# A chain's lower part on GpSimd instead of VectorE, and a smaller booked cost of a new chain, in a two-layer attention and MLP kernel

## The chip, the cores and the metric

The kernel runs on one core of a Trainium2 chip. The metric is the device time of one execution in microseconds. The profile is of one execution, taken by the hardware profiler; times in it are counted from the start of its span. Engines are called PE (TensorE), PEld (its weight loads), DVE (VectorE), ACT (ScalarE), POOL (GpSimd) and SP (SyncE).

## The reference

Two rounds of an attention block and an MLP, each with a layer norm ahead of it and a residual sum behind it, on 2048 rows of 512 in bf16; 32 heads of 16, a hidden width of 1792, the same weights in both rounds:

```python
def _A_ref(x, wqkv, wo):          # x: 1 x 2048 x 512, H = 32, Dh = 16
    qkv = (x @ wqkv) ...          # split into q, k, v per head
    scores = jnp.einsum("bhqd,bhkd->bhqk", q, k) * (Dh ** -0.5)
    p = _softmax(scores, axis=-1)
    o = jnp.einsum("bhqk,bhkd->bhqd", p, v)
    return o ... @ wo

def _B_ref(x, w1, w2):            # w1: 512 x 1792
    return maximum(x @ w1, 0) @ w2

x = x + _A_ref(_layernorm(x), A_wqkv, A_wo)
x = x + _B_ref(_layernorm(x), B_w1, B_w2)
x = x + _A_ref(_layernorm(x), A_wqkv, A_wo)
x = x + _B_ref(_layernorm(x), B_w1, B_w2)
```

## The kernel before

The exponential of the scores is the bulk of the work: 2 x 32 heads x 2048 x 2048 values. They are computed with the keys on the partitions, in blocks of 128 keys by 512 queries (narrower chunks of queries near the end of the second round are packed to 512 columns). A **slot** is three such blocks in three banks of PSUM, of which there are two sets (`ps_s`, slots alternate). In every slot TensorE makes the scores (line 1694), ScalarE takes the exponential of two or three of the blocks into `e` (line 1707), and TensorE multiplies the result by the values into `ps_o` (line 1163, the function `pv`; the values carry a column of ones, which gives the softmax's sum). The scores of slot n+2 go into the banks of slot n, so they wait until its readers are done.

In many slots VectorE takes the third block in ScalarE's place. It uses an approximation that reads a linear function of the score as the bits of a bf16 number. For each block, `lin` = max(score + bias, 0) as int16 (line 1283, PSUM to SBUF, 512 columns). Three blocks make a **chain** (`GROUP` = 3), whose 1536 columns are then shifted up and down: `up` = max(lin + 41, 0) and `down` = max(lin - 41, 0) (both in line 1335, the local function `shifted`). TensorE adds up all three for each block: `lin` and `up` against the values (`vaug`), and `down` against values scaled by 1.55 (`vscaled`). Where no scaled values are there for all blocks of the chain (`p["scaled"]` false), VectorE scales `down` itself (line 1340, `weigh`), and TensorE uses `vaug`. So a block done in this way needs three matmuls against the values instead of one. There are four buffers of `lin` (`NP`) and two each of `up` and `down` (`NC`).

The order of all engines' work is written out when the program is built, by a planner with its own clocks: `now_pe`, `now_dve`, the ends of the exponentials, the time at which SP's queue and GpSimd come free (`sp_free`, `pool_free`), and a table `made` that holds for each result the engine and the planned time. For every slot it puts the matmuls that fit before the scores are needed; `run_dve` then fills VectorE up to the planned end of the exponential before: first the steps that must be done (`musts`: `lin`, and the copies out of `ps_o`), then results of other matmuls, then tasks of `dve_q` whose dependences are planned as met. A task of a chain has the lowest rank unless its head is nearly over. Nothing of this order changes at run time; engines wait for one another by semaphores.

A chain is begun in a slot only if `lin`'s buffer is free, TensorE's other work isn't behind (`pace`, `press`), and

```python
queued = sum(t["cost"] for t in dve_q if "chain" in t)
ends = max(now_dve[0] + others, now_pe[0] + FILL) + SPREAD * (queued + CHAIN)
if asked or now_dve[0] + waiting < now_pe[0] + BACKLOG:
    ... ends < now_pe[0] + till * QS * 0.84 - 1300.0
```

where `till` counts the blocks of the head that are still to come, `SPREAD` is 1.3 and `CHAIN` is the booked cost of a chain in ns. A `down` task has to wait for `("free", "down", n - NC)`: the last matmul on the buffer's content of two chains before.

GpSimd has little to do: the small steps between a norm's statistics and its reciprocal root (lines 587 to 595, nine steps of 128x4 values, 17 times), some copies and fills at the start (lines 207, 236, 243), and the DMAs that spread the reciprocals of the softmax sums (line 1117). `recip` and `rstd` book these on `pool_free`.

Of the kernel before, what the change touches and what calls it, by code (L numbers as in the profile page):

```python
# [17 lines left out]
ALU = mybir.AluOpType  # L18
# [7 lines left out]
def kernel(  # L26
# [10 lines left out]
    nc = tc.nc  # L37
# [28 lines left out]
    THIRD, WEIGHT, SUM = 41.0, 1.55, 3.63198  # L66
# [1 line left out]
    UNIT = 128.0  # L68
    EXP_BIAS = (127.0 - math.log2(SUM)) * UNIT
    GROUP = 3  # L70
    CHAIN = 1500.0
    FILL = 4000.0
    SOON = 1500.0
    NP = 4
    NC = 2
# [4 lines left out]
    PE_TO_DVE, DVE_TO_PE, ACT_TO_PE, PE_TO_ACT = 220.0, 180.0, 160.0, 222.0  # L80
# [6 lines left out]
    BOTH = 4  # L87
    WHOLE = 4
    STARTS, MORE, ORDER = {}, {}, {}
    X_AT = (8.3, 8.5, 9.5, 10.6, 11.0, 11.4, 11.8, 12.1, 12.5, 12.8, 13.3, 14.0)  # L90
    WQ_AT, WV_AT = {0: 0.0, 1: 10600.0, 2: 16000.0, 3: 17400.0}, 10200.0
    FIRST_TRANSPOSE = 1600.0
# [24 lines left out]
    def sb(shape, dt, name):  # L117
        return persist.tile(shape, dt, name=name)
# [40 lines left out]
    up = [sb([P, GROUP * QS], I16, f"up{n}") for n in range(NC)]  # L159
    down = [sb([P, GROUP * QS], I16, f"down{n}") for n in range(NC)]  # L160
# [125 lines left out]
    now_dve = [0.0]  # L286
# [5 lines left out]
    made = {}  # L292

    def mark(key, engine="dve", lag=0.0):
        made[key] = (engine, (now_pe if engine == "pe" else now_dve)[0] + lag)
# [3 lines left out]
    pool_free = [0.0]  # L299
# [27 lines left out]
    def pe_start(kind, ready=0.0):  # L327
        return max(now_pe[0] + (SWITCH if MODE[mode[0]] != MODE[kind] else 0.0), ready)
# [19 lines left out]
    dve_q = []  # L348
    maker = {}
# [3 lines left out]
    def task(cost, fn, makes=(), deps=(), place=None):  # L353
        t = {"cost": cost, "fn": fn, "makes": makes, "deps": deps}
        dve_q.insert(len(dve_q) if place is None else place, t)
        maker.update({k: t for k in makes})
# [921 lines left out]
    def dve_block(half, taken, src, ex, recent):  # L1278
# [3 lines left out]
        def first_step():  # L1282
            first = nc.vector.tensor_scalar(  # L1283
                out=lin[which][:, half * QS : (half + 1) * QS], in0=src, scalar1=EXP_BIAS,
                scalar2=0.0, op0=ALU.add, op1=ALU.max,
            )
            tc.declare_no_dep(
                first.ins, ex.ins, reason="both only read the scores, and in different banks"
            )
            for earlier in recent:  # L1290
                tc.declare_no_dep(
                    first.ins, earlier,
                    reason="the scores read here were written after it, and are waited for",
                )
            step1_end[slot[0]] = now_dve[0]
            readers[slot_no % 2].append((first.ins, (W - 1,)))
            mark(line_key)
            if half == GROUP - 1:
                chain(pairs[-1])
# [26 lines left out]
    def chain(p):  # L1326
        key, n = p["key"], p["n"]
        line = lin[n % NP][:]
        p["scaled"] = all(
            ("third", sg["l"], kb) in made for us in p["blocks"] for sg, kb, g in us  # L1330
        )
        quick = 67 + 0.2591 * GROUP * QS

        def shifted(out, by):
            nc.vector.tensor_scalar(  # L1335
                out=out, in0=line, scalar1=by, scalar2=0.0, op0=ALU.add, op1=ALU.max
            )

        def weigh(x):
            nc.vector.tensor_scalar(out=x, in0=x, scalar1=WEIGHT, scalar2=None, op0=ALU.mult)  # L1340

        above, below = up[n % NC][:], down[n % NC][:]
        first = ("lower",) if not p["scaled"] else ("down",)
        steps = [
            (("up",), lambda: shifted(above, THIRD), [("free", "up", n - NC)]),
            (first, lambda: shifted(below, -THIRD), [("free", "down", n - NC)]),
        ]
        if not p["scaled"]:
            steps.append((("down",), lambda: weigh(below.bitcast(BF16)), [key + first]))
        for of, fn, deps in steps:  # L1350
            task(quick, fn, [key + of], [d for d in deps if d[0] != "free" or d[2] > 0])
            maker[key + of]["chain"] = p
# [12 lines left out]
    for e in range(2):  # L1365
        nc.vector.tensor_reduce(
            out=mask[e],
# [4 lines left out]
            out=qmask[:, e : e + 1],  # L1372
# [4 lines left out]
            out=qmask[:, e : e + 1], in0=qmask[:, e : e + 1], scalar1=SCALE * LOG2E * UNIT, scalar2=None,  # L1377
            op0=ALU.mult,
# [3 lines left out]
    for n in range(2):  # L1382
# [3 lines left out]
        for i in rows:  # L1386
            nc.vector.bn_aggr(out=mv[0][:, i, :], in_=stats[0][:, i, :])
        nc.vector.tensor_scalar(
            out=half_va[n][:], in0=mv[0][:, rows.start : rows.stop, 1], scalar1=EPS, scalar2=None,
            op0=ALU.add,  # L1390
        )
        nc.gpsimd.tensor_tensor(
            out=half_ya[n][:], in0=half_va[n][:], in1=masks[:, 4:5].to_broadcast((P, HALF)),
# [6 lines left out]
    def head_bank(n, w):  # L1400
        return ps_s[n][:, w, :] if n < 2 else ps_f[:]
# [53 lines left out]
    for e in range(2):  # L1455
        uses(
            nc.vector.tensor_scalar(
                out=qbuf[0][:, e, :], in0=head_bank(0, 0), scalar1=qmask[:, e : e + 1],
                scalar2=None, op0=ALU.mult,
# [8 lines left out]
    made["wv",] = "dve", WV_AT  # L1468
    for n, when in enumerate(X_AT):
        made["x", TPC + n] = "dve", 1000.0 * when  # L1470
# [71 lines left out]
    while units:  # L1542
# [5 lines left out]
        for (sg, kb, g), *_ in banked:  # L1548
            if sg["n"] not in seen:
                seen.add(sg["n"])  # L1550
                n = sg["n"] + 1
# [14 lines left out]
        if len(banked) == W and (  # L1566
# [5 lines left out]
            elif asked != 0 and lin_free(pair_no[0] + 1 - NP) and (  # L1572
# [12 lines left out]
                )  # L1585
                ends = max(now_dve[0] + others, now_pe[0] + FILL) + SPREAD * (queued + CHAIN)
                if asked or now_dve[0] + waiting < now_pe[0] + BACKLOG:
# [93 lines left out]
        start = pe_start("s", s_ready)  # L1681
# [7 lines left out]
        for _ in range(times):  # L1689
            pe_run("s", 1, s_ready)  # L1690
            for a, (sg, kb, g) in sorted(zip(place, now), key=in_turn):
# [6 lines left out]
                    start=True, stop=True, tile_position=(32 * g, 0),  # L1698
# [6 lines left out]
        while len(pend) == NE:  # L1705
            force_v()
        ex = nc.scalar.activation(  # L1707
            out=eb[:, 0 : place[m]], in_=b[:, 0 : place[m]], func=ACTF.Exp,
# [33 lines left out]
        if to_load and no >= FIRST_LOAD and sp_free[0] < now_pe[0]:  # L1742
            out, in_ = to_load.popleft()
# [28 lines left out]
    def at_bank(b):  # L1772
        n, w = b
        return ps_s[n][:, w, :] if n < 2 else (ps_f, ps_o)[n - 2][:]
# [68 lines left out]
    for i in rows:  # L1843
        nc.vector.bn_aggr(out=mv[n_last][:, i, :], in_=stats[n_last][:, i, :])
    nc.vector.tensor_scalar(
        out=va_[n_last][:, 0:n_rows], in0=mv[n_last][:, 0:n_rows, 1], scalar1=EPS, scalar2=None,
        op0=ALU.add,
    )
    nc.gpsimd.tensor_tensor(
        out=ya_[n_last][:, 0:n_rows], in0=va_[n_last][:, 0:n_rows],  # L1850
# [29 lines left out]
    for ft in range(NF + LOOK):  # L1880
# [4 lines left out]
        if ft < NF:  # L1885
# [6 lines left out]
            if ft % 2:  # L1892
                out = nc.scalar.activation(out=ht[ft][:, at_column : at_column + width], in_=at_bank(b)[:, 0:width], func=ACTF.Relu)
            else:
                out = nc.vector.tensor_scalar(
                    out=ht[ft][:, at_column : at_column + width], in0=at_bank(b)[:, 0:width],
                    scalar1=0.0, scalar2=None, op0=ALU.max,
                )
# [42 lines left out]
```

## Time and profile before

| | us |
|---|---|
| median of 3 runs (1455.55 to 1455.71) | 1455.7 |
| the profiled execution | 1454.99 |
| its span | 1453.1 |
| ACT busy | 1426.5 |
| PE busy | 1368.8 |
| DVE busy | 1307.2 |
| POOL busy | 96.7 |

The span runs from the first to the last instruction; the profiled execution's own time lies 1.9 us above it. Busy time is summed over the whole span, with stages that have different limits. The granted TensorE clock is 1.00 throughout. The page's line of a group gives its source line, engine, operation, what is written and read with shapes, the count, busy us in all, the mean in ns, and the idle time of the engine ahead of it with what ended it. One line of the source can stand for several tiles: 1335 for `up` and `down`, 1163 for all products with the values.

### The profile page before, as it was taken

What the parts mean: (1) busy time and instruction counts of PE and PEld (TensorE: products, weight loads), DVE (VectorE), ACT (ScalarE), POOL (GpSimd) and SP (SyncE); (2) the same over time, 40 slices, a digit from 0 to 9 for tenths busy, and PEclk for the clock granted to TensorE, in tenths of its full rate; (3) what the DMA queues carried; (4) which work ended last, traced back from release to release, by engine and by line L of the source; (5) the groups of instructions that cost most, each with busy time, mean ns of one, the idle gap of its engine ahead of it and who ended that gap; (6) DMA issues with size and microseconds to landing.
All of it is one profiled execution on the core that took longest, in us unless ns stands there. A gap on an engine that the chain in (4) does not pass through costs nothing.

```text
span 1453.1 us, 47371 instructions
## 1 busy us (share of the span) xinstructions
PE 1368.8 (94%) x20884; PEld 511.7 (35%) x20885; DVE 1307.2 (90%) x2414; ACT 1426.5 (98%) x1386; POOL 96.7 (7%) x249
## 2 busy tenths in 40 slices
PE   8999899999999999999999999889999999999898
PEld 3222222222232223222222223223234444545665
DVE  7969999999999999999599987899989799998864
ACT  7999999999999999999999999999999999999996
POOL 5000001001010011000000000001001010010000
PEclk9999999999999999999999999999999999999999
DMA  5201101101012100210101100000110211223030
GB/s 146 82 5 24 25 10 31 42 14 31 10 24 50 27 17 10 46 39 17 24 5 26 35 5 5 10 15 18 45 39 20 54 29 39 51 45 69 11 70 18
DMA packets 135502, 46.59 MB, mean 32 GB/s; under 512 B 119904, under 2 KB 132512, under 8 KB 135296
## 3 DMA queue, kind: packets, MB, share of 16 engines
q1 hardware_dynamic: 128240, 37.44, 10.8%
q0 software_dynamic: 5568, 5.15, 1.9%
q8 instruction: 163, 2.67, 0.8%
q10 hardware_dynamic: 1488, 0.98, 0.2%
q14 instruction: 43, 0.35, 0.1%
HBM read 24.38 MB, written 2.10 MB: 18 GB/s over the span
## 4 chain that ended last, share of the span: by engine, by line
ACT 76%; PE 17%; DVE 5%; issue 1%; DMA 0%; DVEq 0%; ACTq 0%
ACT e L1707 76%; PE ps_s L1694 5%; PE ps_f L542 5%; PE ps_o L1163 5%; DVE lin L1283 2%; PE ps_s L1778 1%; DVE down L1335 1%; DVE up L1335 1%; DVE vaug L776 0%; DVE x L909 0%; DVE ht L869 0%; DVE stats L578 0%; DMA x<-in_A_x_dram 0%; DVE u L1055 0%; PE ps_o L542 0%
## 5 line engine op out<-in xcount | busy, mean ns | idle before, releaser
L1707 ACT ACTIVATE e<-ps_s 128x1024 bf16<-128x1024 f32 (+1 forms) x1366 | 1418.0, 1207 | 7.9 <-PE ps_s L1694 5.4
L1283 DVE TENSOR_SCALAR lin<-ps_s 128x512 int16<-128x512 f32 x993 | 663.7, 683 | 34.8 <-PE ps_s L1694 29.0
L1694 PE MATMUL ps_s<-q,ktp 32*128 32x512 bf16 (+2 forms) x6346 | 578.6, 321 | 52.9 <-ACT e L1707 47.3
L1163 PE MATMUL ps_o<-e,vaug 128*32 128x512 bf16 (+2 forms) x4318 | 389.4, 326 | 8.1 <-DVE r L1055 3.5
L1694 PEld LDWEIGHTS <-ktp 32*128 32x128 bf16 x6346 | 183.5, 91 | 523.4 <-issue 507.0
L1163 PEld LDWEIGHTS <-vaug 128*32 128x32 bf16 x7153 | 177.4, 95 | 225.2 <-issue 194.6
L1335 DVE TENSOR_SCALAR up<-lin 128x1536 int16<-128x1536 int16 x331 | 182.0, 550 | 14.9 <-PE ps_o L1163 13.6
L1335 DVE TENSOR_SCALAR down<-lin 128x1536 int16<-128x1536 int16 x331 | 181.6, 549 | 0.5 <-PE ps_o L1163 0.5
L1163 PE MATMUL ps_o<-up,vaug 128*32 128x512 bf16 (+2 forms) x1314 | 168.7, 328 | 0.9 <-issue 0.9
L1163 PE MATMUL ps_o<-lin,vaug 128*32 128x512 bf16 (+2 forms) x1314 | 158.5, 328 | 2.4 <-DVE u L1055 0.7
L1163 PE MATMUL ps_o<-down,vscaled 128*32 128x512 bf16 (+2 forms) x1107 | 152.3, 335 | 0.0
L542 PE MATMUL ps_f<-w,ht 128*32 128x512 bf16 x1680 | 135.0, 382 | 0.9 <-DVE x L909 0.7
L542 PE MATMUL ps_f<-xnT,w 128*32 128x512 bf16 (+1 forms) x1792 | 124.3, 355 | 1.2 <-DVE ht L869 0.5
L542 PE MATMUL ps_f<-xnT,wkq 128*32 128x512 bf16 (+2 forms) x1376 | 101.6, 353 | 7.7 <-DVE vaug L776 2.2
L869 DVE TENSOR_SCALAR ht<-ps_f 128x512 bf16<-128x512 f32 (+1 forms) x111 | 74.1, 667 | 19.6 <-PE ps_f L542 12.6
L1163 PEld LDWEIGHTS <-vscaled 128*32 128x32 bf16 x1107 | 50.2, 96 | 18.0 <-issue 10.7
L542 PEld LDWEIGHTS <-w 128*32 128x32 bf16 x1792 | 41.3, 95 | 39.6 <-issue 28.6
L542 PEld LDWEIGHTS <-ht 128*32 128x32 bf16 x1680 | 37.2, 95 | 39.8 <-issue 27.1
L542 PEld LDWEIGHTS <-wkq 128*32 128x32 bf16 x1376 | 33.3, 95 | 42.4 <-issue 33.2
L587 POOL TENSOR_TENSOR ta<-stats 128x4 f32<-128x4 f32 (+2 forms) x17 | 4.8, 281 | 604.0 <-DVE stats L578 604.0
L578 DVE BATCH_NORM_STATS2 stats<-x 128x6 f32<-128x512 bf16 x63 | 42.3, 682 | 1.4 <-DMA x<-in_A_x_dram 1.1
L542 PE MATMUL ps_f<-wv,xnT 128*32 128x512 bf16 x480 | 38.6, 383 | 3.1 <-DVE vaug L776 1.7
(140 smaller groups left out, 583.5 us busy)
## 6 DMA issues: line engine op xcount, KB each, us to landing
w<-in_B_w_dram SPq DMA_DIRECT2D x144, 128.0 KB
q<-xn SPq DMA_DIRECT2D x48, 64.0 KB
out_dram<-x SPq DMA_DIRECT2D x15, 128.0 KB
x<-in_A_x_dram SPq DMA_DIRECT2D x14, 128.0 KB
u<-r POOLq DMA_DIRECT2D x12, 128.0 KB, 4.6
ktp<-in_B_w_dram SPq DMA_DIRECT2D x10, 128.0 KB
u<-ht POOLq DMA_DIRECT2D x6, 128.0 KB, 4.7
r<-r SPq DMA_DIRECT2D x6, 128.0 KB
```

The costliest lines, as they stand in the source:

```text
L542: nc.tensor.matmul(out[cols], lhsT[:, cols], rhs, start=i % k == 0, stop=i % k == k - 1, tile_position=(0, 32 * g), skip_group_check=True,)
L578: nc.vector.bn_stats(out=stats[ln_n(tag)][:, i, :], in_=x_t[tt][:])
L587: pool.tensor_tensor(out=t1, in0=st[:, :, 1], in1=st[:, :, 4], op=ALU.subtract)
L869: nc.vector.tensor_scalar(out=out, in0=sums, scalar1=0.0, scalar2=None, op0=ALU.max)
L1163: nc.tensor.matmul(ps_o[32 * g : 32 * g + 32, 0 : sg["w"]], values[:, 4 * sg["T"] + g, 2 * e : 2 * e + 32], rhs, start=g not in sg["begun" ...
L1283: first = nc.vector.tensor_scalar(out=lin[which][:, half * QS : (half + 1) * QS], in0=src, scalar1=EXP_BIAS, scalar2=0.0, op0=ALU.add, op1 ...
L1335: nc.vector.tensor_scalar(out=out, in0=line, scalar1=by, scalar2=0.0, op0=ALU.add, op1=ALU.max)
L1694: score = nc.tensor.matmul(b[:, a : a + sg["w"]], kt[32 * g : 32 * g + 32, kc : kc + P], qbuf[sg["n"] % 2][32 * g : 32 * g + 32, sg["e"], ...
L1707: ex = nc.scalar.activation(out=eb[:, 0 : place[m]], in_=b[:, 0 : place[m]], func=ACTF.Exp, scale=1.0 / (LOG2E * UNIT),)
L1778: uses(nc.tensor.matmul(out, lhsT, rhs, start=first, stop=last), b, needs=needs)
```

## The change

When an `up` has been put on VectorE, the new function `up_step` looks whether GpSimd can make `down` out of it: max(up - 82, 0), which is the same number as max(lin - 41, 0). It does so where the chain's blocks all have scaled values, the buffer of `down` is planned to be free, and GpSimd could start within 600 ns (`POOL_WAIT`) of VectorE's planned time. Then the `down` task is taken out of VectorE's queue, GpSimd is booked for 2300 ns (`POOL_DOWN`) from a start 150 ns (`POOL_LAT`) behind `up` or later, and `down` is marked as made at the end of that. Else VectorE makes it as before. `CHAIN` goes from 1500 to 1100. `POOL_SPACE` is not used.

```diff
-    CHAIN = 1500.0
+    CHAIN = 1100.0
...
+    POOL_DOWN, POOL_LAT, POOL_WAIT, POOL_SPACE = 2300.0, 150.0, 600.0, 0.0
...
+        def up_step():
+            shifted(above, THIRD)
+            free = ("free", "down", n - NC)
+            if not p["scaled"] or n > NC and free not in made:
+                return
+            start = max(now_dve[0] + POOL_LAT, pool_free[0], made.get(free, (0, 0.0))[1] + DVE_TO_PE)
+            if start > now_dve[0] + POOL_WAIT:
+                return
+            nc.gpsimd.tensor_scalar(
+                out=below, in0=above, scalar1=-2.0 * THIRD, scalar2=0.0, op0=ALU.add, op1=ALU.max
+            )
+            pool_free[0] = start + POOL_DOWN
+            dve_q.remove(maker[key + ("down",)])
+            mark(key + ("down",), lag=pool_free[0] - now_dve[0])
...
         steps = [
-            (("up",), lambda: shifted(above, THIRD), [("free", "up", n - NC)]),
+            (("up",), up_step, [("free", "up", n - NC)]),
             (first, lambda: shifted(below, -THIRD), [("free", "down", n - NC)]),
```

## The prediction

> **What bounds the kernel now.** I read the page's busy line first, then the groups by form, the chain that ended last, and the table by stretches of 50 us.
>
> ```profile
> PE 1368.8 (94%) x20884; PEld 511.7 (35%) x20885; DVE 1307.2 (90%) x2414; ACT 1426.5 (98%) x1386; POOL 96.7 (7%) x249
> ...
> ACT 76%; PE 17%; DVE 5%; issue 1%; DMA 0%; DVEq 0%; ACTq 0%
> ```
>
> ScalarE is busy for 98% of the span and is 76% of the chain that ended last: the exponentials set the time. The groups by form (count, busy us, mean ns, idle before) say how VectorE shortens them:
>
> ```profile
> L1707 ACT ACTIVATE e<-ps_s 128x1024 bf16<-128x1024 f32 x993 | 937.6, 1094 | 4.3 <-PE ps_s L1694 3.5
> L1283 DVE TENSOR_SCALAR lin<-ps_s 128x512 int16<-128x512 f32 x993 | 663.7, 683 | 34.8 <-PE ps_s L1694 29.0 <-ACT e L1707 0.4
> L1707 ACT ACTIVATE e<-ps_s 128x1536 bf16<-128x1536 f32 x372 | 525.7, 1509 | 3.6 <-PE ps_s L1694 1.8 <-PE ps_o L1163 0.8
> L1335 DVE TENSOR_SCALAR up<-lin 128x1536 int16<-128x1536 int16 x331 | 182.0, 550 | 14.9 <-PE ps_o L1163 13.6
> L1335 DVE TENSOR_SCALAR down<-lin 128x1536 int16<-128x1536 int16 x331 | 181.6, 549 | 0.5 <-PE ps_o L1163 0.5
> ```
>
> There are 1366 slots: 993 in which VectorE takes one block of 512 (three make a chain, so 331 chains), 372 in which ScalarE does all 1536 (and one narrow). Start to start in the timeline an exponential takes 904 ns at 1024 and 1331 ns at 1536 (medians), so one block moved is worth 0.427 us and one chain 1.28 us of ScalarE. Is VectorE what limits the number of chains? Not everywhere (columns: stretch, length, then PE, PEld, DVE, ACT, POOL busy):
>
> ```profile
> 250.00:300.00 50.00, 48.83 (x619) 14.06 (x612) 49.80 (x90) 50.00 (x53) 2.53 (x4) 1.00 0.21 47
> 450.00:500.00 50.00, 49.43 (x625) 14.74 (x626) 49.74 (x90) 50.00 (x52) 1.21 (x2) 1.00 0.17 39
> 850.00:900.00 50.00, 47.41 (x600) 15.16 (x597) 36.72 (x65) 48.24 (x44) 2.60 (x9) 1.00 0.02 7
> ```
>
> In some 19 of 29 such stretches (950 us, VectorE 48.3 of 50 on average) VectorE is full; in the others (850:900) the planner's other conditions hold chains back, and a freer VectorE brings nothing. In the full stretches TensorE has only 0.5 to 4 us left too.
>
> **How much goes to GpSimd.** Of 331 chains 40 have the weighing step (line 1340) and stay. For the other 291 I laid the diff's conditions on the starts in the trace: the last read of the `down` buffer two chains before lies behind, and GpSimd, 2.3 us per piece, comes free within 0.6 us. 239 pass. A `down` starts 0.46 us before what follows it (550 ns long, its end overlaps), so 239 x 0.46 = 110 us leave VectorE.
>
> **What the planner does with it.** `CHAIN` 1100 for 1500 lowers the expected end of a new chain by 1.3 x 400 = 520 ns, and the removed tasks lower its VectorE clock; so it begins k more chains. Each costs VectorE three `lin` at a pitch of 0.60, an `up` of 0.46 and a quarter of a `down`: 2.4 us. If the planner keeps VectorE at its present 96.6% in the full stretches (77% of the chains, so 85 us leave there): 918 - 85 + 2.4k = 0.966 x (950 - 1.28k), k = 23. ScalarE: -29 us; VectorE: +55 us. TensorE: six more matmuls of four abreast per chain, 1.5 x 0.216 = 0.32 us, 7 us in all, which its gaps hold except in stretches such as 450:500; there the new chain makes TensorE late, at most those 7 us.
>
> **The price of one piece on GpSimd.** No row shows a 128x1536 arithmetic step there. Nearest from below is the fill (0.83 ns per element beyond 0.1 us: 1.4 us for 1536); nearest in kind is the copy, which also reads and writes:
>
> ```profile
> L207 POOL COPY wkq<-w 128x512 bf16<-128x512 bf16 x6 | 4.4, 764 | 4.8 <-DMA w<-in_A_wqkv_dram 4.8
> L236 POOL MEMSET q<- 128x1024 bf16 x1 | 1.0, 951 | 0.0
> ```
>
> The copy's slope is (764 - 190)/512 = 1.12 ns (190 is what the smallest GpSimd steps take), 1.9 us for 1536; back to back copies start 0.68 us apart, which gives 2.0. I take 2.0, with 1.4 and 2.3 (the diff's `POOL_DOWN`) as ends.
>
> **What it does to VectorE meanwhile.** This decides the case. Where one of VectorE's int16 steps runs, GpSimd's small steps get longer (start, length):
>
> ```profile
> 223.00 0.54 DVE L1335 TENSOR_SCALAR up<-lin 128x1536 int16<-128x1536 int16 x1
> 223.17 0.43 POOL L587 TENSOR_TENSOR ta<-stats 128x4 f32<-128x4 f32 x1 [46.35 <-DVE stats L578]
> 223.46 0.56 DVE L1335 TENSOR_SCALAR down<-lin 128x1536 int16<-128x1536 int16 x1
> 223.69 0.39 POOL L588 TENSOR_TENSOR ta<-ta 128x4 f32<-128x4 f32 x1
> ...
> 1195.38 1.33 POOL L1117 DMA_DIRECT2D u<-r  x2 [3.14 <-DVE down L1335]
> 1195.77 0.69 DVE L1340 TENSOR_SCALAR down<-down 128x1536 bf16<-128x1536 bf16 x1
> ```
>
> Alone they take 0.20 us. Here each ends 0.05 to 0.06 us after the VectorE step: the second comer waits for the first. The other way, GpSimd first, shows in small: an `up` that began 16 ns behind a GpSimd step took 595 ns instead of 550, and the weighing at 1195.77 took 687. Against it: an `up` at 226.16 inside a 1.04 us power step of four elements per row took 548; but that step hardly moves data. A piece of 1536 elements moves data from end to end, so I take it that a VectorE int16 or bf16 step from SBUF to SBUF (`up`, `down`, `xn`, lines 629 and 1137) that starts within it waits for its end. `lin` reads PSUM, and I charge it nothing.
>
> The Trainium skill, "SBUF — State Buffer", section "Who interferes with whom", says just this: VectorE and GpSimd share one pair of ports as an exclusive lock, and against a VectorE instruction in a two-port mode whoever is first has it for the whole instruction. The rows above agree for GpSimd as second comer; for a long GpSimd step no run here shows it. By that rule the blocking below is in full; by the 45 ns of the small steps alone it would be nearly nothing.
>
> I took the VectorE starts of the trace, removed the 239 `down`s, moved up what stood right behind each, and let every such step wait for a GpSimd piece that had begun. At 2.0 us per piece 130 steps wait, 117 us together; at 1.4 us 84 steps, 51 us; at 2.3 us 180 steps, 172 us. The waits are spread evenly, about 9 us per 100. So of the 110 us freed, VectorE gets nothing at 2.0.
>
> Who is behind the waiting `up`? The next `lin`, and behind it TensorE's scores two slots on: from the end of a `lin` to those scores is 0.55 us in the median, and the scores end 0.30 us before ScalarE needs them. A wait of up to 0.85 us is covered; the 130 waits exceed that by 32 us in sum (5 at 1.4, 60 at 2.3). That is the lower bound. Upper bound: VectorE is already full, catches up nothing, and the 950 us last as long as it needs: 918 - 85 + 55 + 0.77 x 117 = 978, at 98.5% busy 993, so +43.
>
> **Sum**, on the profiled execution (1454.99 us; its span is 1453.1, and 1.9 lies around it; the median of the runs is 1455.7): between 32 - 29 = +3 and +43. I take the middle, +23: 1478. With the ends of the price: 1.4 us gives 5 - 29 = -24, 2.3 us gives (918 - 85 + 55 + 132)/0.985 - 950 = +86.
>
> What is moved past other queues: 46 DMA issues and 17 groups of nine small steps stand in GpSimd's queue and can now stand 2 us behind a piece. The planner books both (`pool_free`), and the ones for `r` are planned 10 us ahead; I cost that at nothing; without that cover a row's normalisation starts 2 us late, 17 times, of which TensorE sees little. SP's queue is not touched.
>
> **Rivals.**
> - Faster: the piece is near the fill's 1.4 us, or does not hold VectorE. Then the 23 chains pay: -24 to -29, 1429. For it: the 548 ns `up` within the power step, and 9 `up`s in 250:290 that mostly lie 3 to 5 us apart. Against: the waits of GpSimd above.
> - Slower by another way: the piece takes over 2.6 us or waits itself, so that it ends later than the planner booked. TensorE's order is fixed, and it reads a `down` 1.9 us after its start in the median (a quarter under 1.2); with a piece 0.5 us over its booking about half of 239 readers wait 0.5 us, 60 us, beside 60 or more of VectorE's: about 1540. It decides from 2.5 us on. GpSimd had to wait behind a VectorE step in only 29 of the 239 cases, 0.4 us each, which speaks against it.
> - Hardly anything happens: conditions fail far more often than in my count, or chains don't increase and waits fall under the cover: 1455.
>
> **Chances.** Forecast 0.55, faster 0.30, late pieces 0.10, nothing 0.05. A measurement of this kernel tells 0.2%, 2.9 us, from no change; the lower bound of the forecast (+3) puts 0.03 of it there. So faster 0.30, same 0.08, slower 0.62. The forecast's own range is 1457 to 1515 (+60, some way from +43 towards the +86 of the longest piece). For 8 in 10 the low end goes down into the faster case, to 1430, which leaves about a third of it (0.10) below; the late pieces (0.10) are left out above.
>
> **What would show it.** In the changed kernel: some 240 `down` rows on POOL of about 2.0 us; `lin` rows some 70 above 993; the shorter exponentials as many more; `up` rows on DVE with a maximum of 2 us or more instead of 595 ns, and a mean above 0.8; new idle time of ScalarE before line 1707, released by TensorE, and of TensorE's scores waiting for `lin`. Wrong: if `up` stays at 550 ns beside running GpSimd pieces, the lock is not there and the time falls. If `up` is long and the time still falls, the cover of 0.85 us was larger than I say. If `down` on POOL lasts over 2.5 us, the second rival is at work.

## The result and the profile after

The changed kernel takes 2062.95 us (median of 4 runs, 2062.38 to 2064.91) against 1455.7: the ratio is 1.4172, 95% interval 1.4151 to 1.4193. The forecast was slower by 23 us; it is slower by 607. The page of the changed kernel, its busy line and the two lines of the groups by form for ScalarE:

```profile
PE 1630.7 (79%) x20735; PEld 533.3 (26%) x20735; DVE 1726.2 (84%) x2299; ACT 1466.3 (71%) x1388; POOL 915.5 (44%) x401
```

```profile
L1723 ACT ACTIVATE e<-ps_s 128x1024 bf16<-128x1024 f32 x1014 | 985.4, 1043 | 472.2 <-PE ps_s L1710 454.2 <-PE ps_o L1164 9.2 <-issue 3.5
L1723 ACT ACTIVATE e<-ps_s 128x1536 bf16<-128x1536 f32 x351 | 495.2, 1476 | 105.6 <-PE ps_s L1710 93.0 <-PE ps_o L1164 5.5 <-issue 5.3
```

The work moved off ScalarE is there: 21 more short exponentials (1014 for 993). But ScalarE, which never waited before (8 us in the same two lines), now stands idle for 578 us, and 547 of them end with the scores from TensorE. VectorE is busy 419 us longer although it does 115 instructions fewer. The groups by form say where:

```profile
L1348 POOL TENSOR_SCALAR down<-up 128x1536 int16<-128x1536 int16 x152 | 823.0, 5414 | 930.9 <-DVE up L1336 734.3 <-PE ps_o L1164 74.7 <-PE ps_s L1710 51.7
L1284 DVE TENSOR_SCALAR lin<-ps_s 128x512 int16<-128x512 f32 x1014 | 678.5, 684 | 153.8 <-PE ps_s L1710 149.0 <-ACT e L1723 0.5
L1336 DVE TENSOR_SCALAR up<-lin 128x1536 int16<-128x1536 int16 x338 | 473.8, 1408 | 38.5 <-PE ps_o L1164 22.2 <-issue 9.0 <-POOL down L1348 4.2
L1336 DVE TENSOR_SCALAR down<-lin 128x1536 int16<-128x1536 int16 x186 | 222.5, 1196 | 8.2 <-PE ps_o L1164 8.1
```

GpSimd made 152 of 338 `down`s and took 5.41 us for each, not 2.0. `up` went from a mean of 550 ns to 1408, the `down`s left on VectorE from 549 to 1196, and `lin`, which reads PSUM, stayed at 684 (683 before). At 550 ns the 338 `up`s would take 186 us and the 186 `down`s 102: 408 us of VectorE's time are waiting that the profile counts as busy. One place in the timeline (start, length):

```profile
381.85 5.37 POOL L1348 TENSOR_SCALAR down<-up 128x1536 int16<-128x1536 int16 x1 [5.39 <-DVE up L1336]
382.49 0.69 DVE L1284 TENSOR_SCALAR lin<-ps_s 128x512 int16<-128x512 f32 x1 [0.80 <-PE ps_s L1710]
383.60 0.69 DVE L1284 TENSOR_SCALAR lin<-ps_s 128x512 int16<-128x512 f32 x1 [0.42 <-PE ps_s L1710]
384.21 3.42 DVE L1336 TENSOR_SCALAR up<-lin 128x1536 int16<-128x1536 int16 x1
387.55 0.67 DVE L1284 TENSOR_SCALAR lin<-ps_s 128x512 int16<-128x512 f32 x1
```

Two `lin` pass beside the piece unhindered; the `up` of the next chain starts 2.36 us into it and ends 0.41 us after it (387.63 against 387.22). The `lin` behind the `up` is 3 us late, and the scores that go into its bank with it. The list of waits (us, times, longest) has ScalarE's waits for scores and, since TensorE's order is fixed, a second, smaller wait that wasn't there before:

```profile
ACT e L1723 <- PE ps_s L1710: 547.2, 368, 5.8
PE ps_o L1164 <- POOL down L1348: 109.2, 57, 3.4
```

The granted TensorE clock, 1.00 before, averages 0.85, and TensorE is busy for 262 us more with about as many products.

### The profile page after: what moved, and what is told of

Same layout as the page of the kernel before. It is cut to its first block, busy times and chain, and to the rows that moved or that the text cites. A ratio compares the mean times of both kernels' runs of the same rounds, so it can differ in the third digit from the quotient of the medians.

```text
span 2063.1 us, 47311 instructions
## 1 busy us (share of the span) xinstructions
PE 1630.7 (79%) x20735; PEld 533.3 (26%) x20735; DVE 1726.2 (84%) x2299; ACT 1466.3 (71%) x1388; POOL 915.5 (44%) x401
## 5 line engine op out<-in xcount | busy, mean ns | idle before, releaser
L1723 ACT ACTIVATE e<-ps_s 128x1024 bf16<-128x1024 f32 (+1 forms) x1366 | 1457.1, 1154 | 577.9 <-PE ps_s L1710 547.2
L1348 POOL TENSOR_SCALAR down<-up 128x1536 int16<-128x1536 int16 x152 | 823.0, 5414 | 930.9 <-DVE up L1336 734.3
L1710 PE MATMUL ps_s<-q,ktp 32*128 32x512 bf16 (+2 forms) x6130 | 666.1, 363 | 107.1 <-DVE lin L1284 77.6
L1336 DVE TENSOR_SCALAR up<-lin 128x1536 int16<-128x1536 int16 x338 | 473.8, 1408 | 38.5 <-PE ps_o L1164 22.2
L1164 PE MATMUL ps_o<-e,vaug 128*32 128x512 bf16 (+2 forms) x4285 | 440.8, 362 | 11.8 <-DVE r L1056 3.4
L1164 PE MATMUL ps_o<-down,vscaled 128*32 128x512 bf16 (+2 forms) x1128 | 186.6, 404 | 147.4 <-POOL down L1348 109.2
L1336 DVE TENSOR_SCALAR down<-lin 128x1536 int16<-128x1536 int16 x186 | 222.5, 1196 | 8.2 <-PE ps_o L1164 8.1
L1164 PE MATMUL ps_o<-lin,vaug 128*32 128x512 bf16 (+2 forms) x1347 | 191.5, 362 | 2.6 <-DVE r L1056 1.7
L543 PE MATMUL ps_f<-xnT,w 128*32 128x512 bf16 (+1 forms) x1792 | 154.6, 417 | 11.3 <-DVE ht L870 7.8
L543 PE MATMUL ps_f<-wo,ot 128*32 128x512 bf16 x496 | 45.8, 445 | 9.5 <-DVE ht L870 4.7
```

Of the source, the lines that this page charges most:

```text
L543: nc.tensor.matmul(out[cols], lhsT[:, cols], rhs, start=i % k == 0, stop=i % k == k - 1, tile_position=(0, 32 * g), skip_group_check=True,)
L1164: nc.tensor.matmul(ps_o[32 * g : 32 * g + 32, 0 : sg["w"]], values[:, 4 * sg["T"] + g, 2 * e : 2 * e + 32], rhs, start=g not in sg["begun" ...
L1336: nc.vector.tensor_scalar(out=out, in0=line, scalar1=by, scalar2=0.0, op0=ALU.add, op1=ALU.max)
L1348: nc.gpsimd.tensor_scalar(out=below, in0=above, scalar1=-2.0 * THIRD, scalar2=0.0, op0=ALU.add, op1=ALU.max)
L1710: score = nc.tensor.matmul(b[:, a : a + sg["w"]], kt[32 * g : 32 * g + 32, kc : kc + P], qbuf[sg["n"] % 2][32 * g : 32 * g + 32, sg["e"], ...
L1723: ex = nc.scalar.activation(out=eb[:, 0 : place[m]], in_=b[:, 0 : place[m]], func=ACTF.Exp, scale=1.0 / (LOG2E * UNIT),)
```

## The experiments

Three theories: A, VectorE's int16 steps stand still beside a GpSimd piece; B, `down` comes later than booked and TensorE's fixed order waits; C, the smaller `CHAIN` begins chains that the order can't carry. The first four runs tell them apart.

**CHAIN alone.** `up_step` is not used; `CHAIN` stays at 1100.

```diff
-            (("up",), up_step, [("free", "up", n - NC)]),
+            (("up",), lambda: shifted(above, THIRD), [("free", "up", n - NC)]),
```

> CHAIN at 1100 as in the change, but VectorE makes every down. Theory A (VectorE's int16 steps stand still while a 5.4 us GpSimd piece runs) and theory B (down comes 3 us later than booked and TensorE's fixed order waits for it): no GpSimd piece, so no loss: 1445 to 1465 us, some 5 to 10 more chains than 331. Theory C (the smaller CHAIN begins chains that the order can't carry): most of the 607 us, over 1700.

1451.5 us, ratio 0.9974 (0.9964 to 0.9983): 334 chains for 331, and 0.3% faster. C is out: the smaller constant costs nothing by itself. (At 930 it is worse again, below.)

**The hold alone.** The order of the kernel before; GpSimd is triggered by a copy of one column of `up` and then works on spare data.

```diff
-    CHAIN = 1100.0
+    CHAIN = 1500.0
...
+            nc.gpsimd.tensor_copy(out=trig[:], in_=above[:, 0:1])
             nc.gpsimd.tensor_scalar(
-                out=below, in0=above, ...
+                out=spare_out, in0=again(spare_in), ...   # 128x1536; the input repeats 32 columns
             )
-            pool_free[0] = start + POOL_DOWN
-            dve_q.remove(maker[key + ("down",)])
-            mark(key + ("down",), lag=pool_free[0] - now_dve[0])
+            pool_own[0] = start + 5500.0                  # only while slot[0] <= 450
```

> The order of the kernel before (CHAIN 1500, VectorE makes every down), and beside it in the first 450 slots GpSimd does a piece of the same form and size (int16, 128x1536, add and max) on spare data behind the ups, at least 5.5 us apart; nobody waits for its result. Theory A: some 60 pieces of 5.4 us; as in the changed kernel about 2.9 us of VectorE waiting per piece, less what is covered (0.85 us): 100 to 190 us more, about 1580 us, and up and down rows of up to 5.8 us in the first 470 us only. Theory B: nobody reads the piece, so within 10 us of 1456, and up and down rows of 550 ns.

1673.39 us, ratio 1.1498 (1.1475 to 1.1521): +218 us for 51 pieces, 4.3 us each, more than A expected. Nobody reads their result. Groups by form:

```profile
L1359 POOL TENSOR_SCALAR ktp_late<-spare_in 128x1536 int16<-128x1536 int16 x51 | 276.0, 5411 | 0.3
L1346 DVE TENSOR_SCALAR down<-lin 128x1536 int16<-128x1536 int16 x331 | 297.8, 900 | 1.1 <-PE ps_o L1174 1.1
L1346 DVE TENSOR_SCALAR up<-lin 128x1536 int16<-128x1536 int16 x331 | 231.8, 701 | 20.7 <-PE ps_o L1174 16.3 <-issue 2.6 <-PE ps_f L553 0.5
L640 DVE TENSOR_SCALAR xn<-x,mv,ya 128x512 bf16<-128x512 bf16 x60 | 26.4, 475 | 1.1 <-POOL ya L1875 0.7 <-POOL ya L606 0.5
```

Against the kernel before, `down` grew by 116 us, `up` by 50 and `xn` (22.1 us there) by 4: 170 us of waiting on VectorE cost 218. In the stretch from 0 to 690 us, which has all the pieces, the clock was 0.85 (1.00 before); behind it, it was 1.00 again.

**The lateness alone.** A power step on 31 spare columns takes the piece's time (5.34 us), and only 32 columns of `down` follow it; the other columns stay zero.

```diff
+            nc.gpsimd.tensor_copy(out=powi[:, 0:1].bitcast(I16)[:, 0:1], in_=above[:, 0:1])
+            nc.gpsimd.tensor_tensor(
+                out=powo[:, 0:31], in0=powi[:, 1:32],
+                in1=masks[:, 4:5].to_broadcast((P, 31)), op=ALU.pow,
+            )
             nc.gpsimd.tensor_scalar(
-                out=below, in0=above, ...
+                out=below[:, 0:32], in0=above[:, 0:32], ...
```

> The changed kernel, but GpSimd's piece is a power step on 128x31 spare values (about 5.4 us, hardly any data moved) and behind it max(up - 82, 0) for the first 32 of 1536 columns; the rest of down is left out (zeros). So down comes as late as in the change, while little of SBUF is touched. Theory A: up and down on VectorE stay near 550 ns; what is left is TensorE's waiting for down: 1460 to 1600. Theory B: as slow as the change, 1900 to 2060.

1846.23 us, ratio 1.2685 (1.266 to 1.2711): +391 for 152 pieces. Neither expectation holds. `up` and `down` took 553 and 550 ns, so there is no hold, as A says; yet the loss is far above A's 1600. The row of `up`, and the waits:

```profile
L1338 DVE TENSOR_SCALAR up<-lin 128x1536 int16<-128x1536 int16 x338 | 184.8, 553 | 140.8 <-POOL down L1355 90.6 <-PE ps_o L1166 38.2 <-issue 8.9
...
PE ps_o L1166 <- POOL down L1355: 220.6, 105, 5.6
...
DVE up L1338 <- POOL down L1355: 90.6, 42, 5.5
```

TensorE waits 221 us for `down`, and VectorE waits 91 us for something I had not thought of: GpSimd reads `up` until its piece ends, and the next but one `up` can't be written into that buffer earlier. What each of the two waits costs by itself, this run does not separate.

**Honest booking.** `POOL_DOWN` 5500 for 2300.

> The changed kernel with POOL_DOWN 5500 in place of 2300, so that the planner books what a piece takes. Theory A: TensorE's waits for down (109 us in the changed kernel) nearly go, the pieces get some fewer (110 to 150), VectorE's waits of 2.9 us per piece stay: 1750 to 1950. Theory B: the booking was the fault, so 1440 to 1550.

1905.7 us, ratio 1.3094 (1.3068 to 1.312): +450 for 102 pieces, 4.4 us each, the price of `lock_alone`. TensorE's waits for GpSimd's `down` fell from 109.2 us to 2.2:

```profile
PE ps_o L1164 <- POOL down L1348: 2.2, 1, 2.2
```

So the hold alone is enough for the whole price per piece (the change pays 607/152 = 4.0). Lateness costs 391/152 = 2.6 us per piece where nothing is held, but these prices leave no room for it on top of the hold: the two losses cover each other and must not be added. The orders of the three kernels differ, so this is a comparison of prices, not of one edit.

**What a step costs on GpSimd.** Eleven steps behind the last output of the kernel before, where VectorE is idle.

> The kernel before, and behind its last output eleven steps on GpSimd with VectorE idle: int16 128x1536 add and max twice, add alone, bf16 add and max, bf16 times a number, bf16 copy, bf16 sum of two tensors, int16 add and max at 512 and at 128 columns, fp32 512 columns add and max, fill. If 5.37 us is the step's own time and not contention: 5.4 us for the first two. If the second operation or int16 is what costs, the add alone or the bf16 one comes near the copy's 1.12 ns per column (1.9 us); if every arithmetic step of this kind costs 3.5 ns per column, all but copy and fill are about 5.4.

One execution, 1492.81 us with the eleven steps; only their lengths are read. The timeline (start, length; two of the same kind are merged):

```profile
1450.41 10.89 POOL L1917 TENSOR_SCALAR lin<-lin 128x1536 int16<-128x1536 int16 x2
1461.38 4.09 POOL L1918 TENSOR_SCALAR lin<-lin 128x1536 int16<-128x1536 int16 x1
1465.56 5.38 POOL L1919 TENSOR_SCALAR lin<-lin 128x1536 bf16<-128x1536 bf16 x1
1471.02 4.12 POOL L1920 TENSOR_SCALAR lin<-lin 128x1536 bf16<-128x1536 bf16 x1
1475.20 1.47 POOL L1921 COPY lin<-lin 128x1536 bf16<-128x1536 bf16 x1
1476.75 3.08 POOL L1922 TENSOR_TENSOR lin<-lin,e 128x1536 bf16<-128x1536 bf16 x1
1479.92 1.93 POOL L1923 TENSOR_SCALAR lin<-lin 128x512 int16<-128x512 int16 x1
```

5.4 us is the step's own time. The second operation costs 1.3 us, bf16 for int16 nothing (5.38), and a plain copy of the same shape takes 1.47. Arithmetic with a constant costs 2.8 times a copy, with two constants 3.7 times.

**The prediction's own price.** GpSimd makes 512 of the 1536 columns, 1.92 us, in the order of the change; the other columns stay zero.

```diff
-                out=below, in0=above, ...
+                out=below[:, 0:512], in0=above[:, 0:512], ...
```

> The changed kernel with its order and bookings, but GpSimd makes only the first 512 of down's 1536 columns; the other 1024 are left out (zeros). At the 3.5 ns per column of the changed kernel a piece is 1.9 to 2.0 us, the price that the prediction took. Theory A with the prediction's own sum at 152 pieces (70 us off VectorE, some 75 waits of 0.9 us, 7 more chains): 1455 to 1490 us; up rows of at most 2.4 us. If the sum itself was wrong beside the price (no cover for a wait, as the 4.3 us per 5.4 us piece of lock_alone says): 1.3 us for each us that VectorE waits, no gain from the freed 70 us: 1520 to 1570.

1454.75 us, ratio 0.9999 (0.9989 to 1.0008). With the same 152 pieces at about 2 us (1.99 on average) the time is that of the kernel before. They are not free: `piece_32` below, with the same order and pieces of 0.3 us, takes 7 us less. But they cost far less than the sum had it. The rows by form, and three pieces with the steps beside them:

```profile
L1336 DVE TENSOR_SCALAR up<-lin 128x1536 int16<-128x1536 int16 x338 | 188.2, 563 | 27.8 <-PE ps_o L1164 16.8 <-POOL down L1348 5.6 <-issue 3.3
L1336 DVE TENSOR_SCALAR down<-lin 128x1536 int16<-128x1536 int16 x186 | 110.2, 592 | 2.5 <-PE ps_o L1164 2.4
```

```profile
163.53 1.92 POOL L1348 TENSOR_SCALAR down<-up 128x512 int16<-128x512 int16 x1 [6.32 <-DVE up L1336]
163.89 0.67 DVE L1336 TENSOR_SCALAR up<-lin 128x1536 int16<-128x1536 int16 x1
```

```profile
608.33 1.92 POOL L1348 TENSOR_SCALAR down<-up 128x512 int16<-128x512 int16 x1 [2.94 <-DVE up L1336]
609.02 0.55 DVE L1336 TENSOR_SCALAR up<-lin 128x1536 int16<-128x1536 int16 x1
```

```profile
205.60 1.92 POOL L1348 TENSOR_SCALAR down<-up 128x512 int16<-128x512 int16 x1 [3.81 <-DVE up L1336]
206.99 0.95 DVE L1336 TENSOR_SCALAR up<-lin 128x1536 int16<-128x1536 int16 x1
```

An `up` that starts 0.36 us into the piece loses 0.12 us, one at 0.69 loses nothing, and one at 1.39 waits until the piece has ended and ends 0.42 us after it. The other steps of this run agree: all 37 `up`s and `down`s that start 0.5 to 1.3 us into a piece take at most 0.56 us, and all 30 that start in its first 0.45 us take longer than that. Here the piece holds VectorE only in its first and its last half microsecond; between them it is free.

**A piece of 32 columns**, mostly 0.32 us: what the idea is worth if GpSimd costs next to nothing. The other columns stay zero.

> The changed kernel with its order and bookings, but GpSimd makes only the first 32 of down's 1536 columns; the rest is left out (zeros). A piece is about 0.31 us (as behind the power steps in late_alone) and hardly holds VectorE. This is what the freed 152 steps are worth if GpSimd costs nothing: 7 more chains than before are 9 us of ScalarE, so 1443 to 1450 us; if the planner's order for the change is bad in itself, over 1460.

1447.71 us, ratio 0.995 (0.9935 to 0.9965), inside the expectation: 7 us is all that the 7 more chains and the 70 us off VectorE bring.

**CHAIN at 930.**

> CHAIN at 930 (what the planner books for the two shifted steps of a chain), VectorE makes every down: the same direction as chain1100_alone, which gained 0.26%: 1448 to 1455 us if more chains still find room on VectorE, over 1456 if VectorE is then late.

1457.77 us, ratio 1.0019 (1.001 to 1.0029), with 329 chains. The constant only nudges the planner, up or down; 1100 alone remains the one version here that does the whole computation faster than both kernels.

**Is it the size of the piece?** `lock_alone` again, each piece cut into three of 512, or two of 768, with the same columns of GpSimd work in the same places.

```diff
-            nc.gpsimd.tensor_scalar(
-                out=spare_out, in0=again(spare_in), ...
+            for c in range(0, GROUP * QS, QS):            # or a step of 768
+                nc.gpsimd.tensor_scalar(
+                    out=spare_out[:, c : c + QS], in0=again(spare_in), ...
```

> lock_alone with each 5.4 us piece of GpSimd written as three of 512 columns one after another (about 5.8 us together, same places, same spare data, nobody waits). Theory A1 (a piece holds VectorE's int16 steps from its start to its end, whatever its size): as lock_alone, 1640 to 1690 us, up and down rows up to 5 us. Theory A2 (from piece_512: a piece of 512 holds them only in its first 0.5 us and its last 0.5 us; only a longer piece holds all the time): waits of at most 0.5 us, covered: 1455 to 1465 us, longest up or down row about 1 us.

> As lock_split, but two pieces of 768 columns (about 2.8 us each). A1: 1640 to 1690 us. A2: if the free middle goes with any size over 512, waits of up to 2.8 us and 1520 to 1600 us; if it only shrinks, waits near 1 us and under 1480 us.

1486.39 us (ratio 1.0213, 1.0198 to 1.0229) and 1489.32 (1.0233, 1.0212 to 1.0253) against 1673.39. A1 is out. A2 has the kind of the waits right (short ones, and for 768 a middle that shrinks and does not vanish), but both times lie above what it allowed. Groups by form of `lock_split`, and a line of its waits:

```profile
L1346 DVE TENSOR_SCALAR down<-lin 128x1536 int16<-128x1536 int16 x331 | 194.7, 589 | 0.5 <-PE ps_o L1174 0.5
L1346 DVE TENSOR_SCALAR up<-lin 128x1536 int16<-128x1536 int16 x331 | 193.0, 584 | 14.5 <-PE ps_o L1174 11.9 <-POOL trig L1358 0.6 <-PE ps_f L553 0.5
...
DVE xn L640 <- POOL ya L606: 6.7, 2, 4.9
```

There are 13 us more on `down` and 11 on `up`: 24 us of short waits, five of them over half a microsecond, the longest 0.8 us. Beside them VectorE's `xn` waits 7 us for a norm's small steps, which stand in GpSimd's queue behind the three pieces (0.5 us in `lock_alone`). Together that is 31 us of VectorE's time, and the cost is 31 us. With pieces of 768 it is 29 us of holds, the longest 1.1 us, and 7 us of `xn`, at a cost of 34. In these pieces (2.77 us) the steps that start in the first 0.65 us or after 2.0 us wait; those between do not, but for two.

**All of `down` in three pieces**, booked at 6.0 us, out of `up`:

> The changed kernel with all of down made on GpSimd, but as three pieces of 512 columns, and booked at 6.0 us (POOL_DOWN) instead of 2.3. A1: as booked_5500, about 1900 us. A2: some 100 chains, each with waits of some 0.1 to 0.3 us that are covered; 46 us come off VectorE for a few more chains: 1445 to 1458 us, about the kernel before or 0.5% better.

1611.21 us, ratio 1.1066 (1.1047 to 1.1084): neither. The holds are short, but the wait for `up`'s buffer, seen first in the lateness run, is back:

```profile
L1336 DVE TENSOR_SCALAR up<-lin 128x1536 int16<-128x1536 int16 x334 | 187.7, 570 | 125.2 <-POOL down L1349 102.4 <-PE ps_o L1164 18.2 <-issue 3.3
```

**The same out of `lin`**, which has four buffers:

```diff
-                    out=below[:, c : c + QS], in0=above[:, c : c + QS], scalar1=-2.0 * THIRD,
+                    out=below[:, c : c + QS], in0=line[:, c : c + QS], scalar1=-THIRD,
```

> three_512, but GpSimd makes down out of lin (four buffers) and not out of up (two): max(lin - 41, 0). In three_512 VectorE's up waited 102 us for GpSimd to have read the buffer of two chains before, and the time was 156 us over the kernel before. If that wait is the cause: it goes from the list of waits, and at 1.3 us for each us 1465 to 1495 us are left, with the 24 us of short holds the rest. If the cause is another (order, bookings): still over 1580 us.

1494.15 us, ratio 1.0265 (1.0248 to 1.0282). The wait for `up`'s buffer is gone from the list, and 117 of the 156 us with it, as expected. The 39 us that are left are near the holds in size: `up` is at 638 ns, 29 us over its time, `down` at 602, 12 over. No run takes these apart from the rest.

## Why the prediction was wrong, point by point

The direction and the mechanism were right: VectorE's int16 steps wait for GpSimd, `lin` does not, and ScalarE then waits for scores. The size was off by a factor of 26. The step that failed first is the price of one GpSimd piece, put at 2.0 us and measured at 5.4; what a wait costs was wrong beside it. By the prediction's own steps:

- **What bounds it now:** right. Most of the 607 us is ScalarE's new waiting for scores, 547 us.
- **The price of one piece (2.0 us, ends 1.4 and 2.3): the step that failed.** It measured 5.37, with VectorE idle too. I took the copy as the row nearest in kind because it reads and writes; but arithmetic with two constants costs 3.7 times as much as a copy. A fit through a row of another operation was no bound. The upper end, the diff's own `POOL_DOWN`, was no measurement either. The condition of my second rival, a piece beyond 2.5 us, was met; I gave it 0.10. Its mechanism, lateness, was not what cost: with it nearly gone, `booked_5500` pays as much per piece. And its 1540 was too low, because I added lateness to waits of 2.6 us pieces.
- **What it does to VectorE meanwhile:** right for the real piece, wrong for the one I had assumed. At 5.37 us a step waits from any point of the piece until its end. The Trainium skill, "SBUF — State Buffer", section "Who interferes with whom", says that whoever comes first has the shared pair of ports for the whole instruction and the other blocks fully. The trace agrees for the long piece; for pieces of 512 and 768 columns it disagrees, since their middle is free, and the measurement decides. So my sum at 2.0 us, 117 us of waits and +23 us, was wrong too, also for 152 pieces in place of 239: `piece_512` has about 4 us more on `up` and 8 on `down`, and 1454.75 us. The two errors lay in opposite directions.
- **The cover of 0.85 us:** wrong. I read it off medians and let every wait use it anew. With VectorE nearly full, a wait is hardly made up before the next: 31 us of waits cost 31 in `lock_split`, and 12 us of holds cost 7 in `piece_512` against `piece_32`. The upper bound's reasoning (VectorE has no room, so every us counts) was the better one, but even it falls short for long waits. 170 us of them cost 218 in `lock_alone`, 1.3 us per us. In the changed kernel `up`, `down`, `xn` and the weighing waited 426 us, and the time rose by 607, 1.4 per us. With 152 pieces (0.77 x 70 = 54 us freed), 7 chains (17 us) and 0.77 x 426 = 328 us of waits the upper bound's own sum gives (918 - 54 + 17 + 328)/0.985 - 950, about +280. So the price of the piece and its waits explain less than half of the 607 by my sum; the rest is what a long wait costs beyond its length. It goes with the lower clock (scores of 512 columns took 436 ns on average instead of 382), but no run separates the two, and this part of the cause stays open.
- **How many pieces and chains:** 239 and 23 were forecast, 152 and 7 came, 3 of the 7 from `CHAIN` alone. I laid the conditions on the measured starts, while the planner decides by its own clocks; no run shows which condition turned the others away. The ideal gain was so 7 us (`piece_32`) and not 29.
- **What else is moved:** costed at nothing was that GpSimd reads `up` for the length of its piece. The wait for the buffer is hidden in the changed kernel (4.2 us), since VectorE stands still then anyway, and comes out when the hold goes (102 us in `three_512`). The queue that I did put at nothing, the norm's small steps behind a piece, was right for the change, where the planner books the pieces (`xn` waits 0.7 us); it costs 7 us in `lock_split`, which doesn't book them.
- The first rival (faster, the piece is short or does not hold) is what `piece_32` shows, at about a quarter of its gain.

## What to carry to other kernels

Before work is moved to an engine that hardly appears in the trace, measure that very operation there, with its type, its size and its number of operands: one run with the step behind the kernel's end would have given 5.4 us. Then ask what it shares with the engine that it is to relieve, and for which of that engine's steps; the loss came to 4 us per piece for a step of 0.46 us moved. And check the lifetime of what the slower engine reads: `up`, which TensorE alone read before, is now also held for the five microseconds of GpSimd's piece. Where the step has to go there all the same, try it in short pieces: the same columns in pieces of 512 cost 31 us instead of 218. In this kernel even that gained nothing: `three_512_lin` is 39 us slower than the kernel before.

## What the runs showed of the hardware

- GpSimd, 128x1536: copy 1.47 us, sum of two tensors 3.08, one operation with a constant 4.1, two 5.4; int16 and bf16 alike. With two constants, 512 columns take 1.92 and 128 take 0.64.
- A GpSimd piece of 512 or 768 columns holds VectorE's int16 steps from SBUF to SBUF only at its two ends (about 0.5 us each of 1.92, 0.65 and 0.75 of 2.77); one of 1536 columns does so for all of its 5.37 us, and the held step ends 0.41 us behind it. A power step of 5.34 us on 31 columns does not hold them (553 and 550 ns). Where between 768 and 1536 the gap closes was not tried.
- VectorE's `lin`, which reads PSUM, ran beside all of these at its usual 680 to 685 ns.
- The profile counts such a hold as busy time of the waiting engine: VectorE's 84% hold 408 us in which `up` and `down` only waited. The mean of a row, not its engine's share, shows it.
